# State products on the quarters of the matmul array, rows turned by the transpose form, and scatters spread, in a kernel of retention and two layers of experts

## The chip, the cores and the metric

The kernel runs on one core of one Trainium2 chip. The metric is the device time of one execution in microseconds (us), as the median of several runs. A core has TensorE (matmuls, PE in the profile; its weight loads have a row of their own, PEld), VectorE (DVE), ScalarE (ACT), GpSimd (POOL) and SyncE (SP), which here only issues transfers. TensorE takes a stationary operand (the weights) from SBUF into its array, streams a moving operand past it and writes to PSUM, which has 8 banks of 512 float32 values for each of 128 partitions.

## The reference

Inputs are q, k and v of shape (8, 8, 576, 64) in float32 and two layers of 8 experts (512 to 1024 to 512). The first step is retention, attention without a softmax and with a decay of its own for each head:

```python
scores = (q @ k^T) / sqrt(64)
ret    = scores * where(i >= j, gamma[h] ** (i - j), 0)
x      = ret @ v                      # then as 4608 rows of 512
logits = x @ w_gate                   # expert of a row: argmax; weight: its softmax
out[t] = gate_w * sigmoid(x @ w_output_gate)[e] * relu(x @ w1[e]) @ w2[e]
```

A second layer of experts of the same form follows, with a bias on its logits that depends on a modality, and without the output gate.

## The kernel before

Two stages follow each other. The first, `attention_and_routing`, computes the retention, the logits of the first layer and each row's place, and scatters the rows to DRAM by expert. The second, `experts`, runs both layers of experts; the diff doesn't touch it.

The first stage works on 36 chunks of 128 rows. Each sequence of 576 has four chunks of 128 and a rest of 64; the rests of two sequences make one chunk, the tail. So of 36 chunks 8 are the first of a sequence, 24 have one chunk before them and 4 are tails. The decay is taken out of the products by scaling v by gamma to the power of minus its position (`vs`, on GpSimd) and the result by gamma to the power of its position (`gx`). What earlier chunks of a sequence add is carried in a state `Sb`, a 64x64 matrix for each head, summed up from chunk to chunk. All of this is in float32; a float32 matmul shows as two rows of PE and two weight loads.

For a chunk TensorE does, by line:

- `scores` (277): 8 products of 64 rows by 128 columns into `pa`, one head each; the two heads of a pair stand on the two halves of the partitions.
- `kv` (284): 8 products with 64 output partitions into `pS`, from which `state` (293 on DVE, 295 on ACT for a first chunk) makes `Sb` in two instructions of 64 partitions. `Sb` has a 128x128 block for a pair of heads, whose two 64x64 corners off the diagonal are zeros, set once.
- `qS` (302): 4 products of the whole array, a pair's block of `Sb` as weights against q, into `po`, one bank. A tail has two such sets of 64 columns, one for each sequence.
- `av` (322): 8 products into the two halves of `po`'s partitions, on top of `qS`.
- `out` (326, DVE) scales `po` into `og`, which has head dimensions in its partitions. `turned` (331) multiplies `og` as weights with `iw`, an identity of 128 columns and 16 columns of both gates beside it, so that one set of 4 float32 products into `px` (two banks) gives the rows and, in four parts, their logits.

Then ACT takes the sum of squares (336), DVE adds up the four parts of the logits (339) and makes a power of two of the sum (345, 349), ACT and DVE write the row as two float16 halves (353, 356).

GpSimd scales v (269, `vs`), zeroes what lies above the diagonal of the scores (317, two instructions a chunk) and issues the scatters of finished rows (178), one a chunk.

Chunks are routed in 9 groups of 4, 5, 4, 5, 4, 5, 4, 3 and 2. `route` is a chain of some 15 small steps on DVE with a few on the other engines (lines 191 to 234; `oh` is 201, `zz` 203). The order of everything is written out: `PLAN` gives each step of chunk i a time i + offset, in chunks, and the program is issued sorted by it; every engine works off its part in that order. On TensorE that is scores of i, `turned` of i - 2, `qS` and `av` of i - 1, `kv` of i. A group's scatters stand at the end of its route plus 0.225, and 0.428 chunks apart.

Of the kernel before, what the change touches and what calls it, by code (L numbers as in the profile page):

```python
# [13 lines left out]
F32 = mybir.dt.float32  # L14
I32 = mybir.dt.int32
AF = mybir.ActivationFunctionType
ALU = mybir.AluOpType
AX = mybir.AxisListType

B, H, S, HD = 8, 8, 576, 64  # L20
D, F, E = 512, 1024, 8
N = B * S
P = 128
C = 128
NCH = 4
# [4 lines left out]
TOK0 = 8192.0  # L30
WS = 64.0
NT = N // P
IW = P + 2 * E

PLAN = {
    "vs": -1.3, "S": 0.0, "x": 2.03, "am0": 0.05, "am1": 0.06, "qS": 1.06, "av": 1.1, "kv": 0.2, "cut0": 0.21, "cut1": 0.22, "oe": 1.3, "Sb": 0.5,
# [2 lines left out]
GATES = -5.2, -1.440, -2.415, 1.091  # L39
WARM = 15  # L40
STEPS, RANKS, STEP, HURRY = 15, 10, 0.1684, {27: 0.1, 31: 0.055, NT - 2: 0.04}
SCATTER = 0.225, 0.428
HALVES = (38.2, 38.3, 38.32, 38.34, 38.36, 38.38, 38.4, 38.42), 43.0
READY = 11

# [1 line left out]
def const_tables():  # L47
    g = 1.0 - 2.0 ** (-5.0 - np.arange(H, dtype=np.float64))
    p = np.arange(P)
    cols = {}  # L50
    for c in range(NCH + 1):
        at = c * C + (p if c < NCH else p % 64) - S // 2
        cols[f"gv{c}"] = g[None, :] ** -at[:, None].astype(np.float64)
    tok = np.zeros((P, NT))
    for b in range(B):
        for c in range(NCH):
            tok[:, tile_index(b, c)] = b * S + c * C + p
    for bp in range(B // 2):
        tok[:, tile_index(2 * bp, NCH)] = 2 * bp * S + 512 + p + 512 * (p >= 64)
    cols["tok"] = tok - TOK0  # L60
    cols["desc"] = np.tile(8.0 - np.arange(E), (P, 1))
    cols["e8"] = np.tile(np.arange(E, dtype=np.float64), (P, 1))
    cols["e40"] = np.tile(R // P * np.arange(E), (P, 1))
    cols["eR"] = np.tile(R * np.arange(E), (P, 1))
    cols["eP"] = np.tile(R * np.arange(E) + P, (P, 1))
    cols["suf"] = np.tile((np.arange(E)[:, None] <= np.arange(E)[None, :]).reshape(1, 64), (P, 1))
    off, at = {}, 0
    for k, v in cols.items():
        off[k] = (at, at + v.shape[1])
        at += v.shape[1]  # L70
    gx = np.zeros((NCH + 1, 2, HD, 4, P))
    for c in range(NCH + 1):
        at = c * C + (p if c < NCH else p % 64) - S // 2
        gx[c] = (g.reshape(4, 2).T[:, None, :, None] ** at.astype(np.float64)) / 8.0
    return np.concatenate(list(cols.values()), 1).astype(np.float32), off, gx.reshape(NCH + 1, P, 4 * P).astype(np.float32)


def tile_index(b, c):

    return (b // 2) * 9 + ((b % 2) * NCH + c if c < NCH else 8)  # L80


def attention_and_routing(tc, st, I, K):

    nc = tc.nc
    pool = lambda n, b: st.enter_context(tc.tile_pool(name=n, bufs=b))
    one, two, three = pool("one", 1), pool("two", 2), pool("three", 3)
    psum = lambda n, b: st.enter_context(tc.tile_pool(name=n, bufs=b, space=bass.MemoryType.PSUM))
    ps = psum("ps", 1)
    rows = dram_disjoint_views(K["xs1"], NT)  # L90
# [8 lines left out]
    id16, mt = (one.tile([P, P], F16, tag=n, name=n) for n in ("id16", "mt"))  # L99
# [18 lines left out]
                rest[w] = r  # L118

    wgf = one.tile([P, 4, 16], F32, tag="wgf", name="wgf")  # L120
    iw = one.tile([P, 4, IW], F32, tag="iw", name="iw")
    wg2f = one.tile([P, 4, 8], F32, tag="wg2f", name="wg2f")
    mi = one.tile([NT, P, 2], I32, tag="mi", name="mi")
    tokm = one.tile([P, NT, XM - 1], F32, tag="tokm", name="tokm")
# [5 lines left out]
        nc.sync.dma_start(mi, I["modality"].bitcast(I32).rearrange("t (p w) -> t p w", w=2))  # L130

    def gate_weights():
        nc.vector.tensor_copy(iw[:, :, 0:P], id16.unsqueeze(1).to_broadcast([P, 4, P]))
        nc.vector.tensor_copy(iw[:, :, P:IW], wgf)
        split3((K["wg2"], wg2f, 8))

    def modalities():

        mf = one.tile([NT, P], F32, tag="mf", name="mf")
        nc.vector.tensor_copy(mf, mi[:, :, 0])  # L140
        pm = ps.tile([P, 1024], F32, tag="px", bufs=2, name="pm_mod")
        id32 = one.tile([NT, NT], F32, tag="id32", name="id32")
        nc.vector.tensor_copy(id32, id16[0:NT, 0:NT])
        nc.tensor.transpose(pm[:, 0:NT], mf, id32)
        nc.vector.tensor_copy(tokm[:, :, 0], col("tok"))
        nc.vector.memset(tokm[:, :, 1:2], 1.0)
        nc.vector.memset(tokm[:, :, 10:11], 0.0)
        return pm[:, 0:NT]
# [88 lines left out]
    gx = [one.tile([P, 512], F32, tag=f"gx{c}", name=f"gx{c}") for c in range(NCH + 1)]  # L237
# [3 lines left out]

    HALF = (slice(0, 64), slice(64, 128))

    states = [one.tile([P, 4, P], F32, tag=f"Sb{n}", name=f"Sb{n}") for n in range(7)]
    for x in states:
        nc.gpsimd.memset(x, 0.0)

    class Chunk:

# [36 lines left out]

        def state(self):
            self.Sb = states[order.index(self) % 7]
            for r in range(2):
                at = lambda x: x[HALF[r], :, r * HD:(r + 1) * HD]  # L290
                new = self.pS[HALF[r], 0:256].rearrange("p (a d) -> p a d", a=4)
                if self.c:
                    nc.vector.tensor_tensor(at(self.Sb), new, at(self.before[0].Sb), op=ALU.add)
                else:
                    nc.scalar.activation(at(self.Sb), new, AF.Copy)

        def qS(self):
            self.po = ps.tile([P, 4, P], F32, tag="po", name=f"po{self.tag}")
            for m, bf in enumerate(self.before):
                part = HALF[m] if self.tail else slice(0, P)  # L300
                for hp in range(4):
                    nc.tensor.matmul(self.po[:, hp, part], bf.Sb[:, hp], self.pairs("q")[:, hp, part], start=(m == 0 and hp == 0), stop=False)

        def a_full(self, r):

# [11 lines left out]
                nc.gpsimd.affine_select(out=d4, in_=d4, pattern=[[0, 4], [1, C]], compare_op=ALU.is_ge, fill=0.0, base=0, channel_multiplier=-1)  # L317

        def av(self):
            for hp in range(4):  # L320
                for r in range(2):
                    nc.tensor.matmul(self.po[HALF[r], hp, :], self.vs[:, 2 * hp + r, :], self.aa[r][:, hp * P:(hp + 1) * P], start=(not self.c and hp == 0), stop=(hp == 3))

        def out(self):
            self.og = two.tile([P, 4, P], F32, tag="og", name=f"og{self.tag}")
            nc.vector.tensor_tensor(self.og, self.po, gx[self.c].rearrange("p (h i) -> p h i", h=4), op=ALU.mult)  # L326

        def turned(self):
            px = ps.tile([P, 1024], F32, tag="px", bufs=2, name=f"px{self.tag}").rearrange("p (h t) -> p h t", h=4)
            for hp in range(4):  # L330
                nc.tensor.matmul(px[:, hp, 0:IW], self.og[:, hp, :], iw[:, hp, :], start=True, stop=True)  # L331
            self.x, self.xl = px[:, :, 0:P], px[:, :, P:IW]

        def squares(self):
            sq = two.tile([P, 512], BF16, tag="sq", name=f"sq{self.tag}")
            nc.scalar.activation(four(sq), self.x, AF.Square, accum_out=self.of("ss"))

        def logits(self):
            nc.vector.tensor_reduce(self.group.lg[:, self.place], self.xl.rearrange("p h e -> p e h"), axis=AX.X, op=ALU.add)

        def of(self, n):
            return getattr(self.group, n)[:, self.place:self.place + 1]
# [7 lines left out]

        def x_hi(self):
            self.xr = self.group.xrow[:, self.place, 0:512].bitcast(F16)
            nc.scalar.activation(four(self.xr[:, 0:512]), self.x, AF.Identity, scale=self.of("sc"))

        def x_lo(self):
            nc.vector.scalar_tensor_tensor(four(self.xr[:, 512:1024]), self.x, self.of("sc"), four(self.xr[:, 0:512]), op0=ALU.mult, op1=ALU.subtract)

    four = lambda a: a.rearrange("p (h d) -> p h d", h=4)
    order = []
    for bp in range(B // 2):  # L360
        order += [Chunk(2 * bp + bb, c) for bb in range(2) for c in range(NCH)] + [Chunk(2 * bp, NCH)]
# [14 lines left out]
    add = lambda when, f, *a_: plan.append((when, len(plan), f, a_))  # L376
# [7 lines left out]
    for gr in groups:  # L384
        last = max(gr.start + n + PLAN["lg"] for n, x in enumerate(gr.items))
        chain = route(gr)
        for k in range(STEPS):
            last += HURRY.get(gr.start, STEP)
            if k == RANKS and gr.start < NT - 2:
                last = int(last - 0.045) + 1.045  # L390
            add(last, next, chain, None)
        for n, x in enumerate(gr.items):
            add(last + SCATTER[0] + n * SCATTER[1], scatter, x)
    def counts():

        pm = ps.tile([P, 512], F32, tag="pS", name="pm_cnt")
# [16 lines left out]
    for when, f in zip(GATES, (gate_loads, gate_weights, lambda: mod.append(modalities()), token_data)):  # L413
        add(when, f)
# [984 lines left out]
def laid_out(inputs):  # L1399

    a = {n: inputs[n] for n in _INS}
    for n in "kv":
        a[n] = by_tile(inputs[n].transpose(0, 2, 1, 3)).reshape(NT, P, D)
    for n, x in (("q", "q"), ("dk", "k")):
        a[n] = by_tile(inputs[x].transpose(0, 2, 1, 3)).reshape(NT, P, 4, P).transpose(0, 3, 2, 1).reshape(NT, P, D)
    a["modality"] = by_tile(inputs["moe2_modality_id"].reshape(B, S))
    rows = lambda w: w.reshape(4, P, E).transpose(1, 0, 2)
    a["gates"] = np.concatenate([rows(inputs["moe_w_gate"]), rows(inputs["moe_w_output_gate"])], 2)
    a["gate2"] = rows(inputs["moe2_w_gate"])
    return a  # L1410

# [16 lines left out]
```

## Time and profile before

| | us |
|---|---|
| median of 3 runs | 1028.07 (1027.68 to 1029.19) |
| the profiled execution, its own time | 1029.08 |
| its span in the trace | 1026.6 |

The trace is of one execution. Its span runs from the first to the last instruction, and 2.5 us of the execution's own time lie outside it. A line of the profile's groups names source line, engine, operation, the tiles that it writes and reads, their shape and how many there were. A matmul's row begins when its moving operand may stream and ends with the last result, so rows overlap and what a matmul costs is read from the start of one row to the start of the next. Brackets behind a row tell how long its engine had been idle and what ended that.

### The profile page before, as it was taken

How to read it: one execution, taken by the hardware profiler on the slowest of the kernel's cores; microseconds unless marked ns; L12 is line 12 of the kernel's file. 1: busy time of each engine (PE TensorE's matmuls, PEld its weight loads, DVE VectorE, ACT ScalarE, POOL GpSimd, SP SyncE). 2: the span in 40 equal slices, each digit the busy share in tenths (PEclk: the TensorE clock that was granted, in tenths of full speed). 3: DMA queues.
4: the chain of work that ended last, by engine and by line, in shares of the span. 5: the costliest groups of instructions: out<-in, count | busy, mean ns of one | idle time of the engine just before them, and what ended most of it. 6: DMA issues, size and time to landing. Idle time of an engine off the chain costs nothing. (4 is left out here: it accounts for less than half of the span.)

```text
span 1026.6 us, 23918 instructions
## 1 busy us (share of the span) xinstructions
PE 984.4 (96%) x8529; PEld 708.7 (69%) x8529; DVE 465.6 (45%) x1420; ACT 358.6 (35%) x701; POOL 234.8 (23%) x308
## 2 busy tenths in 40 slices
PE   8998999399999999999999999999999999999996
PEld 6998898357667676767666767666776666776673
DVE  4666766666565656565656565323111111111111
ACT  3564554344444444343534343223111121111111
POOL 6566655510121111111112111101100101100110
PEclk9999999789999999999999999999999999999998
DMA  8887875279739383747665564361222211112100
GB/s 326 302 295 245 276 246 177 96 238 269 187 60 244 76 234 84 190 114 172 216 169 142 111 185 97 113 173 53 52 42 51 72 34 52 53 41 62 52 31 24
DMA packets 180256, 145.10 MB, mean 141 GB/s; under 512 B 136569, under 2 KB 136733, under 8 KB 180128
## 3 DMA queue, kind: packets, MB, share of 16 engines
q1 hardware_dynamic: 171168, 114.89, 42.2%
q0 software_dynamic: 8960, 28.62, 7.4%
q8 instruction: 67, 1.10, 0.4%
q14 instruction: 61, 0.50, 0.2%
HBM read 80.46 MB, written 33.92 MB: 111 GB/s over the span
## 5 line engine op out<-in xcount | busy, mean ns | idle before, releaser
L991 PE MATMUL ph<-xT,wb 128*128 128x256 f16 (+2 forms) x1344 | 338.0, 262 | 0.1
L993 PE MATMUL ph<-xT,wb 128*128 128x256 f16 (+2 forms) x1344 | 338.0, 262 | 0.0
L992 PE MATMUL ph<-xT,wb 128*128 128x256 f16 (+2 forms) x1344 | 338.0, 262 | 0.0
L1205 DVE SCALAR_TENSOR_TENSOR hT<-ph,hT 128x512 f16<-128x512 f32 (+2 forms) x168 | 105.8, 637 | 332.2 <-DVEq L457 332.1
L1001 PE MATMUL py<-wb,hT 128*128 128x512 f16 x608 | 230.4, 379 | 0.0
L1000 PE MATMUL py<-wb,hT 128*128 128x512 f16 x608 | 230.3, 379 | 0.0
L999 PE MATMUL py<-wb,hT 128*128 128x512 f16 x608 | 230.3, 379 | 0.0
L1093 ACT ACTIVATE hT<-ph 128x512 f16<-128x512 f32 (+2 forms) x168 | 92.4, 551 | 200.9 <-ACTq L457 200.7
L991 PEld LDWEIGHTS ph<-xT,wb 128*128 128x128 f16 x1344 | 131.3, 98 | 16.3 <-issue 0.4
L992 PEld LDWEIGHTS ph<-xT,wb 128*128 128x128 f16 x1344 | 131.3, 98 | 16.0
L993 PEld LDWEIGHTS ph<-xT,wb 128*128 128x128 f16 x1344 | 131.4, 98 | 12.7
L1331 POOL DMA_INDIRECT out_dram<-yo,idxo x37 | 35.9, 969 | 334.3 <-POOLq L457 334.3
L1001 PEld LDWEIGHTS py<-wb,hT 128*128 128x128 f16 x608 | 59.4, 98 | 71.8
L999 PEld LDWEIGHTS py<-wb,hT 128*128 128x128 f16 x608 | 59.3, 98 | 63.4
L1000 PEld LDWEIGHTS py<-wb,hT 128*128 128x128 f16 x608 | 59.4, 98 | 63.2
L1320 POOL TENSOR_SCALAR idx<-v_pos 128x1 int32<-128x1 f32 x39 | 22.2, 570 | 325.8 <-POOLq L457 325.8
L469 DVE SCALAR_TENSOR_TENSOR wb<-stg,wb 128x2048 f16<-128x2048 f32 x38 | 86.9, 2287 | 10.2 <-DVEq L457 9.7
L1087 ACT ACTIVATE yo<-py,v_gcol 128x512 f32<-128x512 f32 x37 | 25.4, 688 | 168.2 <-ACTq L457 168.2
L1070 ACT ACTIVATE wb<-stg 128x2048 f16<-128x2048 f32 x38 | 72.3, 1902 | 0.9 <-ACTq L457 0.9
L1324 POOL DMA_INDIRECT xs<-x2row,idx x39 | 44.4, 1137 | 37.5 <-POOLq L457 37.5
L331 PE MATMUL px<-iw,og 128*128 128x144 f32 x288 | 46.0, 304 | 6.7 <-DVE og L326 6.7
L1084 ACT ACTIVATE x2row<-py,v_s 128x512 f16<-128x512 f32 x39 | 26.8, 687 | 71.6 <-ACTq L457 71.6
(152 smaller groups left out, 977.0 us busy)
## 6 DMA issues: line engine op xcount, KB each, us to landing
stg<-in_moe_w_dram SPq DMA_DIRECT2D x38, 1024.0 KB, 5.0
qn<-in_q_dram SPq DMA_DIRECT2D x36, 256.0 KB, 5.0
dkn<-in_dk_dram SPq DMA_DIRECT2D x36, 256.0 KB, 5.1
vn<-in_v_dram SPq DMA_DIRECT2D x36, 256.0 KB, 5.1
kn<-in_k_dram SPq DMA_DIRECT2D x32, 256.0 KB, 5.1
xs<-zero SPq DMA_DIRECT2D x8, 262.0 KB, 2.2
xs<-zero SPq DMA_DIRECT2D x8, 258.0 KB, 2.4
w0s<-in_moe_w_dram SPq DMA_DIRECT2D x8, 256.0 KB, 5.8
```

The source lines that it names most:

```text
L331: nc.tensor.matmul(px[:, hp, 0:IW], self.og[:, hp, :], iw[:, hp, :], start=True, stop=True)
L469: r = fn(*a, **kw).then_inc(self.sem, 1)
L991: pe.matmul(o, w1(P_, 0)[:, c, fs], xT[s][:, c, cs], start=(c == 0), stop=False)
L992: pe.matmul(o, w1(P_, 0)[:, c, fs], xT[s][:, 4 + c, cs], start=False, stop=False)
L993: m = pe.matmul(o, w1(P_, 1)[:, c, fs], xT[s][:, c, cs], start=False, stop=(c == 3))
L999: pe.matmul(py[b], hT[:, 0, f, bs], w2(P_, 0)[:, f, :], start=(f == 0), stop=False)
L1000: pe.matmul(py[b], hT[:, 0, f, bs], w2(P_, 1)[:, f, :], start=False, stop=False)
L1001: m = pe.matmul(py[b], hT[:, 1, f, bs], w2(P_, 0)[:, f, :], start=False, stop=(f == 7))
L1070: ac.activation(wb[P_ % 2][:, 0, 2048 * c:2048 * c + 2048], stg[:, 2048 * c:2048 * c + 2048], AF.Copy, scale=WS).then_inc(T["cv_full"])
L1093: ac.activation(hT[:, 0, 2 * g:2 * g + 2, cs], ph[g][:, :, cs], AF.Relu).then_inc(T["hh_full"])
L1205: stt(hT[:, 1, 2 * g:2 * g + 2, cs], ph[g][:, :, cs], 0.0, hT[:, 0, 2 * g:2 * g + 2, cs], op0=ALU.max, op1=ALU.subtract).then_inc(T["h_full"])
L1324: po.indirect_dma_start(out=xs2, out_offset=bass.IndirectOffsetOnAxis(ap=idx[b], axis=0), in_=x, in_offset=None, bounds_check=E * R - 1, o ...
```

## The change

- `Sb` has 4 x 64 columns with no zeros; `state` is one instruction of 128 partitions by 256.
- `qS` becomes 8 products of 64x64 (16 in a tail), each on one quarter of the array: r picks the half of its rows (and of q's and `Sb`'s partitions), s the half of its columns (and of `po`'s partitions). `po` takes two banks, one for each r. `av` and `out` follow that layout; `gx` and the gates' rows are arranged for it on the host.
- `turned` is four transposes of `og` against a float32 identity `idf` into `px`, which is one bank, and four products of `og` with the 16 gate columns that add up in a bank `pl` of their own. `logits` is a copy of 16 columns.
- A group's scatters stand 0.9 chunks apart, from the group that starts at chunk 22 on 0.428 as before.
- The zeroing of the states at the start goes.

```diff
-SCATTER = 0.225, 0.428
+SCATTER, APART, LATE = 0.225, (0.9, 0.428), 22
...
-    gx = np.zeros((NCH + 1, 2, HD, 4, P))
+    gx = np.zeros((NCH + 1, 2, HD, 2, 2, P))
+    by_place = g.reshape(2, 2, 2).transpose(1, 2, 0)[:, None, :, :, None]
...
-    iw = one.tile([P, 4, IW], F32, tag="iw", name="iw")
+    idf = one.tile([P, P], F32, tag="idf", name="idf")
...
-    states = [one.tile([P, 4, P], F32, tag=f"Sb{n}", name=f"Sb{n}") for n in range(7)]
-    for x in states:
-        nc.gpsimd.memset(x, 0.0)
+    states = [one.tile([P, 4 * HD], F32, tag=f"Sb{n}", name=f"Sb{n}") for n in range(7)]
...
-            for r in range(2):
-                at = lambda x: x[HALF[r], :, r * HD:(r + 1) * HD]
-                new = self.pS[HALF[r], 0:256].rearrange("p (a d) -> p a d", a=4)
-                if self.c:
-                    nc.vector.tensor_tensor(at(self.Sb), new, at(self.before[0].Sb), op=ALU.add)
-                else:
-                    nc.scalar.activation(at(self.Sb), new, AF.Copy)
+            new = self.pS[:, 0:4 * HD]
+            if self.c:
+                nc.vector.tensor_tensor(self.Sb, new, self.before[0].Sb, op=ALU.add)
+            else:
+                nc.scalar.activation(self.Sb, new, AF.Copy)
+
+        def at(self, r, s, u):
+
+            return self.po[HALF[s], 512 * r + P * u:512 * r + P * (u + 1)]
 
         def qS(self):
-            self.po = ps.tile([P, 4, P], F32, tag="po", name=f"po{self.tag}")
+            self.po = ps.tile([P, 1024], F32, tag="po", name=f"po{self.tag}")
             for m, bf in enumerate(self.before):
                 part = HALF[m] if self.tail else slice(0, P)
-                for hp in range(4):
-                    nc.tensor.matmul(self.po[:, hp, part], bf.Sb[:, hp], self.pairs("q")[:, hp, part], start=(m == 0 and hp == 0), stop=False)
+                for u in range(2):
+                    for r, s in ((0, 0), (1, 1), (0, 1), (1, 0)):
+                        hp = 2 * u + s
+                        nc.tensor.matmul(self.at(r, s, u)[:, part], bf.Sb[HALF[r], hp * HD:(hp + 1) * HD], self.pairs("q")[HALF[r], hp, part],
+                                         start=(m == 0 and u == 0), stop=False)
...
         def turned(self):
-            px = ps.tile([P, 1024], F32, tag="px", bufs=2, name=f"px{self.tag}").rearrange("p (h t) -> p h t", h=4)
+            px = ps.tile([P, 512], F32, tag="px", bufs=2, name=f"px{self.tag}")
+            pl = ps.tile([P, 512], F32, tag="pl", name=f"pl{self.tag}")
+            turned = px.rearrange("p (u s r d) -> p r u s d", u=2, s=2, r=2)
+            for n in range(4):
+                nc.tensor.transpose(turned[:, n // 2, n % 2], self.og[:, n, :], idf)
             for hp in range(4):
-                nc.tensor.matmul(px[:, hp, 0:IW], self.og[:, hp, :], iw[:, hp, :], start=True, stop=True)
-            self.x, self.xl = px[:, :, 0:P], px[:, :, P:IW]
+                nc.tensor.matmul(pl[:, 0:2 * E], self.og[:, hp, :], wgf[:, hp, :], start=(hp == 0), stop=(hp == 3))
+            self.x, self.xl = px, pl[:, 0:2 * E]
...
         def logits(self):
-            nc.vector.tensor_reduce(self.group.lg[:, self.place], self.xl.rearrange("p h e -> p e h"), axis=AX.X, op=ALU.add)
+            nc.vector.tensor_copy(self.group.lg[:, self.place], self.xl)
...
         for n, x in enumerate(gr.items):
-            add(last + SCATTER[0] + n * SCATTER[1], scatter, x)
+            add(last + SCATTER + n * APART[gr.start >= LATE], scatter, x)
```

## Rows read from the trace of the kernel before

**Rows 1.** Busy time by stretch: length, PE, PEld, DVE, ACT, POOL, granted clock, DMA share, GB/s.

```profile
20.00:75.00 55.00, 55.00 (x773) 50.82 (x769) 36.29 (x112) 31.67 (x71) 33.00 (x42) 1.00 0.87 306
75.00:92.00 17.00, 14.18 (x167) 12.93 (x163) 14.48 (x35) 6.10 (x16) 8.84 (x12) 0.90 0.64 221
```

**Rows 2.** TensorE's timeline: start us, us, what; chunks at 31, 39 to 46, 50 us.

```profile
30.92 1.25 PE L331 MATMUL px<-iw,og 128*128 128x144 f32 x8
32.09 1.09 PE L322 MATMUL po<-a,vs 128*64 128x128 f32 x16
...
39.32 1.25 PE L331 MATMUL px<-iw,og 128*128 128x144 f32 x8
...
41.69 1.09 PE L322 MATMUL po<-a,vs 128*64 128x128 f32 x16
42.61 0.64 PE L284 MATMUL pS<-vs,kn 128*64 128x64 f32 x16
43.18 1.16 PE L277 MATMUL pa<-qn,dkn 64*128 64x128 f32 x16
44.27 1.25 PE L331 MATMUL px<-iw,og 128*128 128x144 f32 x8
45.35 1.05 PE L302 MATMUL po<-qn,Sb 128*128 128x128 f32 x8
46.34 1.09 PE L322 MATMUL po<-a,vs 128*64 128x128 f32 x16
...
49.54 1.89 PE L302 MATMUL po<-qn,Sb 128*128 128x64 f32 x16
51.36 1.09 PE L322 MATMUL po<-a,vs 128*64 128x128 f32 x16
```

**Rows 3.** The same view where lines 322 and 284 meet, early in the stage.

```profile
15.11 0.28 PE L284 MATMUL pS<-vs,kn 128*64 128x64 f32 x2
15.21 0.27 PE L322 MATMUL po<-a,vs 128*64 128x128 f32 x1
```

**Rows 4.** By line: duration ns min/median/max, first and last start, forms.

```profile
L144 PEld LDWEIGHTS pm_mod<-id,mf x1: 135/135/135, 6.9 to 6.9; 36*128 36x128 f32 x1
L144 PE MATMUL pm_mod<-id,mf x1: 248/248/248, 6.9 to 6.9; 36*128 36x36 f32 x1
...
L277 PEld LDWEIGHTS pa<-qn,dkn x576: 182/188/188, 8.1 to 179.3; 64*128 64x128 f32 x192
L277 PE MATMUL pa<-qn,dkn x576: 272/272/373, 8.1 to 179.4; 64*128 64x128 f32 x192
...
L284 PE MATMUL pS<-vs,kn x512: 219/222/270, 9.9 to 178.3; 128*64 128x64 f32 x171
```

**Rows 5.** TensorE's timeline in the second stage: float16, 256 columns.

```profile
211.31 0.27 PE L992 MATMUL ph<-xT,wb 128*128 128x256 f16 x1
211.42 0.27 PE L993 MATMUL ph<-xT,wb 128*128 128x256 f16 x1
```

**Rows 6.** The timeline around two halts of TensorE, 75 to 90 and 128 us.

```profile
75.75 1.25 PE L331 MATMUL px<-iw,og 128*128 128x144 f32 x8
...
77.70 3.79 DVE L201 TENSOR_TENSOR oh<-wq,m 128x32 f16<-128x32 f32 x1
...
80.40 1.04 POOL L269 TENSOR_TENSOR vs<-vn,cst 128x512 f32<-128x512 f32 x1
...
82.85 1.25 PE L331 MATMUL px<-iw,og 128*128 128x144 f32 x8 [2.38 <-DVE og L326]
...
89.91 1.25 PE L331 MATMUL px<-iw,og 128*128 128x144 f32 x8
...
128.19 1.53 PE L331 MATMUL px<-iw,og 128*128 128x144 f32 x8 [2.09 <-DVE og L326]
```

**Rows 7.** GpSimd's groups, 17 to 188 us: busy us, mean ns, idle before.

```profile
L317 POOL TENSOR_SCALAR_AFFINE_SELECT a<-a 128x512 f32<-128x512 f32 x62 | 38.1, 641 | 28.4 <-ACT a L311 28.2
...
L178 POOL DMA_INDIRECT xs<-xr,pi x32 | 32.0, 1001 | 36.7 <-DVE xr L234 28.3 <-issue 5.0 <-ACT xr L353 3.1
```

More of the change, by code (lines that the diff above doesn't have):

```diff
@@ L32 @@
 NT = N // P
-IW = P + 2 * E
 PLAN = {
@@ L70, in const_tables @@
         at += v.shape[1]
-    gx = np.zeros((NCH + 1, 2, HD, 4, P))
+    gx = np.zeros((NCH + 1, 2, HD, 2, 2, P))
+    by_place = g.reshape(2, 2, 2).transpose(1, 2, 0)[:, None, :, :, None]
     for c in range(NCH + 1):
         at = c * C + (p if c < NCH else p % 64) - S // 2
-        gx[c] = (g.reshape(4, 2).T[:, None, :, None] ** at.astype(np.float64)) / 8.0
+        gx[c] = (by_place ** at.astype(np.float64)) / 8.0
     return np.concatenate(list(cols.values()), 1).astype(np.float32), off, gx.reshape(NCH + 1, P, 4 * P).astype(np.float32)
@@ L132, in gate_weights @@
     def gate_weights():
-        nc.vector.tensor_copy(iw[:, :, 0:P], id16.unsqueeze(1).to_broadcast([P, 4, P]))
-        nc.vector.tensor_copy(iw[:, :, P:IW], wgf)
+        nc.vector.tensor_copy(idf, id16)
         split3((K["wg2"], wg2f, 8))
@@ L140, in modalities @@
         nc.vector.tensor_copy(mf, mi[:, :, 0])
-        pm = ps.tile([P, 1024], F32, tag="px", bufs=2, name="pm_mod")
+        pm = ps.tile([P, 512], F32, tag="px", bufs=2, name="pm_mod")
         id32 = one.tile([NT, NT], F32, tag="id32", name="id32")
@@ L319, in av @@
         def av(self):
-            for hp in range(4):
+            for u in range(2):
                 for r in range(2):
-                    nc.tensor.matmul(self.po[HALF[r], hp, :], self.vs[:, 2 * hp + r, :], self.aa[r][:, hp * P:(hp + 1) * P], start=(not self.c and hp == 0), stop=(hp == 3))
+                    for s in range(2):
+                        hp = 2 * u + s
+                        nc.tensor.matmul(self.at(r, s, u), self.vs[:, 2 * hp + r, :], self.aa[r][:, hp * P:(hp + 1) * P], start=(not self.c and u == 0), stop=(u == 1))
         def out(self):
             self.og = two.tile([P, 4, P], F32, tag="og", name=f"og{self.tag}")
-            nc.vector.tensor_tensor(self.og, self.po, gx[self.c].rearrange("p (h i) -> p h i", h=4), op=ALU.mult)
+            halves = lambda a: a.rearrange("p (r x) -> p r x", r=2)
+            nc.vector.tensor_tensor(self.og.rearrange("p (r u) t -> p r (u t)", r=2), halves(self.po)[:, :, 0:2 * P], halves(gx[self.c]), op=ALU.mult)
         def turned(self):
-            px = ps.tile([P, 1024], F32, tag="px", bufs=2, name=f"px{self.tag}").rearrange("p (h t) -> p h t", h=4)
+            px = ps.tile([P, 512], F32, tag="px", bufs=2, name=f"px{self.tag}")
[3 more added lines that the diff above has]
+                nc.tensor.transpose(turned[:, n // 2, n % 2], self.og[:, n, :], idf)
             for hp in range(4):
-                nc.tensor.matmul(px[:, hp, 0:IW], self.og[:, hp, :], iw[:, hp, :], start=True, stop=True)
-            self.x, self.xl = px[:, :, 0:P], px[:, :, P:IW]
+                nc.tensor.matmul(pl[:, 0:2 * E], self.og[:, hp, :], wgf[:, hp, :], start=(hp == 0), stop=(hp == 3))
+            self.x, self.xl = px, pl[:, 0:2 * E]
         def squares(self):
             sq = two.tile([P, 512], BF16, tag="sq", name=f"sq{self.tag}")
-            nc.scalar.activation(four(sq), self.x, AF.Square, accum_out=self.of("ss"))
+            nc.scalar.activation(sq, self.x, AF.Square, accum_out=self.of("ss"))
         def logits(self):
-            nc.vector.tensor_reduce(self.group.lg[:, self.place], self.xl.rearrange("p h e -> p e h"), axis=AX.X, op=ALU.add)
+            nc.vector.tensor_copy(self.group.lg[:, self.place], self.xl)
         def of(self, n):
@@ L352, in x_hi @@
             self.xr = self.group.xrow[:, self.place, 0:512].bitcast(F16)
-            nc.scalar.activation(four(self.xr[:, 0:512]), self.x, AF.Identity, scale=self.of("sc"))
+            nc.scalar.activation(self.xr[:, 0:512], self.x, AF.Identity, scale=self.of("sc"))
         def x_lo(self):
-            nc.vector.scalar_tensor_tensor(four(self.xr[:, 512:1024]), self.x, self.of("sc"), four(self.xr[:, 0:512]), op0=ALU.mult, op1=ALU.subtract)
-    four = lambda a: a.rearrange("p (h d) -> p h d", h=4)
+            nc.vector.scalar_tensor_tensor(self.xr[:, 512:1024], self.x, self.of("sc"), self.xr[:, 0:512], op0=ALU.mult, op1=ALU.subtract)
     order = []
@@ L1407, in laid_out @@
     rows = lambda w: w.reshape(4, P, E).transpose(1, 0, 2)
-    a["gates"] = np.concatenate([rows(inputs["moe_w_gate"]), rows(inputs["moe_w_output_gate"])], 2)
+    placed = lambda w: w.reshape(2, 2, 2, HD, E).transpose(1, 3, 2, 0, 4).reshape(P, 4, E)
+    a["gates"] = np.concatenate([placed(inputs["moe_w_gate"]), placed(inputs["moe_w_output_gate"])], 2)
     a["gate2"] = rows(inputs["moe2_w_gate"])
```

## Prediction

> **What bounds the kernel now.** First I read the busy time by stretch [rows 1]. From 20 to 75 us, in the first stage, TensorE is busy for 55.00 of 55.00 us at the full clock (granted 1.00, so 2.4 GHz), while VectorE has 36.29, GpSimd 33.00 and ACT 31.67. So this stage goes at TensorE's pace, and the diff touches no other. From 75 to 92 us it is not so: 14.18 of 17.00, at a mean clock of 0.90.
>
> Second, TensorE's timeline [rows 2], where a step costs from its start to the next one's start. A normal chunk is av 41.69 to 42.61 = 0.92, kv 0.57, scores 1.09, turned 44.27 to 45.35 = 1.08, qS 45.35 to 46.34 = 0.99: 4.65 us. With a group's rank products in between it is 4.95 (39.32 to 44.27). A tail's qS, twice as many rows of half the columns, takes 49.54 to 51.36 = 1.82. In a first chunk, without qS, turned is followed at once by av and takes 1.17 (30.92 to 32.09) and not 1.08. The 0.09 more is what it costs to go from a whole-array step to one on halves of the array; qS ends in such a change too. So its 8 rows take (0.99 - 0.09) / 8 = 0.112 each, and the tail's 16 take (1.82 - 0.09) / 16 = 0.108 though they stream 64 columns and not 128. Those rows are bound by loading 128 columns of float32 weights, not by streaming.
>
> Third, what two halves of the array do. av has 16 rows of 128 columns in 0.92 us: two at a time, 8 steps of some 0.11 and a first load of weights. kv's 16 rows of 64 columns take 0.57, (0.57 - 0.09) / 8 = 0.06 a step. The halves don't keep step by construction: kv starts on one half at 15.11 before the other has begun its last av row at 15.21 [rows 3]. So each part of the array works off its own rows.
>
> Fourth, the halts [rows 6]. `oh`, 32 elements wide, lasts 3.79 us and ends at 81.49, just after GpSimd's `vs` ends at 81.44. VectorE's `og` stands behind it in order, and TensorE waits 2.38 us for that; after the wait the clock falls, to a mean of 0.90 over the stretch [rows 1]. From 75.75 to 89.91 are 14.16 us for a normal chunk and one with ranks, 4.65 + 4.95 = 9.60: the halt costs 4.56. A second, with 2.09 of waiting at 128.19, is put at 4.56 x 2.09 / 2.38 = 4.0. In the old order four or five scatters stand within two chunks, 2.3 a chunk, and GpSimd then needs 2 x 0.64 + 1.04 + 2.3 x 1.0 = 4.6 us a chunk [rows 6, 7], as long as the chunk itself. It runs without a break, and by these rows a VectorE step like `oh`, which reads two operands from SBUF, gets through only in a break.
>
> **The change part by part.**
>
> *qS on quarters.* Each quarter has 2 products, so 4 rows of 128 columns, and 64 columns of weights, half the load. No row shows four quarters at once. The bounds come from av: if the four work off their own rows as its two halves do, 4 steps of 0.11; if only two run at a time, 8 steps. I take the first, by [rows 3] and because each half of rows and each half of columns is already seen at work in scores and av. Added are 0.09 for the change into av as before, 0.05 for the first weights (below) and 0.02 for four starts: 0.44 + 0.16 = 0.60 against 0.99, -0.39 in each of 24 chunks. In a tail each quarter has 8 rows of 64 columns: 8 x 0.06 + 0.16 = 0.64 against 1.82, -1.18, four times. With two at a time: 1.04 and 1.12.
>
> *Turned.* The gates' products keep `og` as weights, so their 8 rows cost the load that binds a tail's qS: 8 x 0.108 = 0.86, nearly the old step. The transposes come on top. The one transpose of the trace [rows 4] has one row where every other float32 product has two. Its weights take 135 ns, against 183 and more for 128 columns elsewhere; a first row that waits for its weights is 373 - 272 = 101 ns longer with 128 columns, so some 50 here. That leaves 198 of its 248 for 36 columns. Ordinary rows go from 222 ns at 64 columns to 272 at 128, 0.8 a column, or 200 at 36: the same pace. So 128 columns cost 0.11, one row each. Bounds: float16 streams 256 columns in 0.11 [rows 5], which makes 0.055; and two rows like other products make 0.22. I take 0.11, the only row of that form. Sum: 4 x 0.11 + 0.05 + 0.86 = 1.35. The next change costs nothing more, since 16 columns have left the array long before the next load is due. So +0.27 in 28 chunks and 1.35 - 1.17 = +0.18 in the 8 first ones.
>
> The Trainium skill ("TensorE: Matmul & The Clock Gate", Terms) says that the transpose mode is 4 times faster for float32 than a plain product. By that a transpose would cost a quarter of two rows, near 0.055, and the sum would be lower by 4 x 0.055 in each chunk; the only row here speaks for half and not a quarter.
>
> *State, out, logits.* One VectorE instruction where there were two, and a copy where there was a sum. VectorE isn't the bound; these cost and give nothing as long as TensorE is. `out` still has kv and scores, 0.57 + 1.09 us, as cover before the next turned. If that cover is gone, each such chunk waits. The logits' single bank `pl` is free a whole chunk before it is needed. The zeroing at the start lies ahead of the first loads: nothing.
>
> *Scatters.* 0.9 chunks apart they are 1.1 a chunk: with 5.0 / 32 = 0.16 of issue each, 2 x 0.64 + 1.04 + 1.1 x 1.16 = 3.6 of some 4.5 us, so GpSimd waits for ACT's scores again in each chunk and VectorE gets its break. Both halts above belong to groups before chunk 22; I take them as gone, -8.6. Bounds: nothing gone, or new halts (below). Scatters from chunk 22 on are as before.
>
> *Sum.* 24 x (-0.39 + 0.27) = -2.9; tails 4 x (-1.18 + 0.27) = -3.6; first chunks 8 x 0.18 = +1.4; halts -8.6: -13.7. The profiled execution's own time is 1029.08 (its span 1026.6 and 2.5 around it), 1.0 above the median of 1028.07. So the median becomes 1014.4, put at 1014.5.
>
> **Rivals.**
>
> *Transposes twice as fast* (0.055, the float16 pace): 36 x 4 x 0.055 = 7.9 less, 1006.5. For it: the weights of the one transpose load in half the usual excess. Against: its 248 ns.
>
> *The halts stay*, because one scatter a chunk is enough to close GpSimd's breaks: 1014.5 + 8.6 = 1023. For it: all that covers `og` after av is 1.66 us, so a block of `oh` well short of 3.79 us would do.
>
> *Two quarters at a time*: 24 x 0.44 + 4 x 0.48 = 12.5 more, 1027, no difference that can be measured.
>
> *More halts, the other side.* Scatters spread over four chunks now lie under the route of the following group, which they did only for two groups before 22. If `oh` or `zz` is caught in each of the five groups 4, 9, 13, 18 and 22, that is 5 x 4.3 = 21 us where I count none: 1035. It decides at four of them: 17 more make 1031.7. Against it: the order leaves GpSimd 0.9 us idle in each chunk, and a scatter is preceded by a gap of its issue.
>
> *A transpose of two rows*: 36 x 4 x 0.11 = 15.8 more, 1030, about the edge.
>
> **How the numbers follow.** Chances: forecast 0.38, fast transposes 0.18, halts stay 0.18, two quarters 0.10, more halts 0.10, two rows or something else that is dear 0.06. 0.2% is 2.1 us, about what a measurement of this kernel can tell from no change. Faster are the first three and some of the fourth, 0.76; same 0.08; slower 0.16. The predicted time is the likeliest case's, 1014.5; the range takes in the first four, from 1004 (fast transposes with the loads a little better hidden) to 1027.
>
> **What would show it.** Right: the rows of 302 start four within some 30 ns and qS takes 0.60; line 331's successor has 4 rows 0.11 apart and 8 rows 0.108 apart; `oh` and `zz` stay under 2 us before chunk 22 and TensorE has no wait of over 1 us for `og` there; the second stage is as long as before. Wrong: qS near 1.04, or transposes with eight rows, or TensorE waiting for `og` in more places than two, or the stage ending later while its matmuls are shorter, with VectorE or GpSimd as what it waits for.

## The result, and the profile after

The changed kernel takes 1012.87 us (median of 4 runs, 1011.63 to 1014.00) against 1028.63 of the kernel before on the same chip (4 runs, 1027.68 to 1029.93): a ratio of 0.9833 [0.9819, 0.9848]. The forecast was 1014.5. In the profiled execution the span goes from 1026.6 to 1009.9 us, 16.7 less; the medians are 15.8 apart.

First the stretches of [rows 1] again: length, PE, PEld, DVE, ACT, POOL, granted clock, DMA share, GB/s.

```profile
20.00:75.00 55.00, 55.00 (x923) 50.78 (x921) 33.26 (x108) 30.11 (x69) 35.26 (x45) 1.00 0.91 315
75.00:92.00 17.00, 17.00 (x298) 15.51 (x297) 10.25 (x39) 8.65 (x20) 12.55 (x16) 1.00 0.84 277
```

TensorE is still busy without a break at the full clock from 20 to 75 us, and now from 75 to 92 as well, where it had 14.18 of 17.00 us and a mean clock of 0.90. VectorE, ACT and GpSimd all have room, so the stage goes at TensorE's pace in both stretches. TensorE's timeline, which answers to [rows 2]:

```profile
31.69 0.66 PE L338 MATMUL px<-idf,og 128*128 128x128 f32 x4
...
33.08 1.09 PE L326 MATMUL po<-a,vs 128*64 128x128 f32 x16
...
40.22 0.66 PE L338 MATMUL px<-idf,og 128*128 128x128 f32 x4
...
41.73 0.67 PE L303 MATMUL po<-qn,Sb 64*64 64x128 f32 x16
...
44.91 0.66 PE L338 MATMUL px<-idf,og 128*128 128x128 f32 x4
45.40 0.96 PE L340 MATMUL pl<-wgf,og 128*128 128x16 f32 x8
46.30 0.67 PE L303 MATMUL po<-qn,Sb 64*64 64x128 f32 x16
46.89 1.09 PE L326 MATMUL po<-a,vs 128*64 128x128 f32 x16
...
50.40 0.69 PE L303 MATMUL po<-qn,Sb 64*64 64x64 f32 x32
51.02 1.09 PE L326 MATMUL po<-a,vs 128*64 128x128 f32 x16
```

From start to start, qS takes 46.30 to 46.89 = 0.59 and a tail's 50.40 to 51.02 = 0.62. The four transposes take 44.91 to 45.40 = 0.49 and the gates' eight rows 45.40 to 46.30 = 0.90. A chunk with ranks is 40.22 to 44.91 = 4.69, where it was 4.95; a normal one, from qS to qS, 41.73 to 46.30 = 4.57, where it was 4.65. Cut down to 46.28 to 46.32 us, the same view has one line of four products:

```profile
46.30 0.34 PE L303 MATMUL po<-qn,Sb 64*64 64x128 f32 x4
```

The four quarters' first rows start within 0.02 us of each other and run together. By line, ns (min/median/max), beside [rows 4]: a transpose has one row (x144 for 36 chunks), and its weights load in 141 ns, against 192 for the same `og` in the gates' products.

```profile
L338 PEld LDWEIGHTS px<-idf,og x144: 137/141/143, 18.0 to 172.2; 128*128 128x128 f32 x144
L338 PE MATMUL px<-idf,og x144: 272/273/329, 18.0 to 172.3; 128*128 128x128 f32 x144
...
L340 PEld LDWEIGHTS pl<-wgf,og x288: 190/192/192, 18.4 to 173.1; 128*128 128x128 f32 x144
```

Where the first halt was [rows 6], the timeline now has the following. GpSimd waits for ACT's scores before each pair of cuts (the brackets), `oh` and `zz` last 0.19 and 0.52 us, and the next `turned` starts without a wait, 4.57 us after the one before.

```profile
75.38 0.66 PE L338 MATMUL px<-idf,og 128*128 128x128 f32 x4
...
76.08 0.19 DVE L200 TENSOR_TENSOR oh<-wq,m 128x32 f16<-128x32 f32 x1
76.22 1.22 POOL L319 TENSOR_SCALAR_AFFINE_SELECT a<-a 128x512 f32<-128x512 f32 x2 [0.57 <-ACT a L313]
...
76.97 0.52 DVE L202 TENSOR_TENSOR zz<-lg,oh 128x32 f32<-128x32 f32 x1
...
79.95 0.66 PE L338 MATMUL px<-idf,og 128*128 128x128 f32 x4
```

**The balance.** A measure that every run below has is the stage, in its one profiled execution, from the first `turned` to the last: before 16.97 to 188.51 = 171.54 us, after 18.00 to 171.96 = 153.96, so 17.6 less. The stage's first `turned` is 1.0 later (the first scores wait 2.38 us for `dkn` instead of 0.97; close_scatters below, which starts with the same steps, has it at 16.80, so this is the run's and not the change's), the way from the last `turned` to the experts' first matmul is 0.8 shorter, and the second stage takes 820.4 instead of 819.8: 17.6 - 1.0 + 0.8 - 0.6 = 16.8, the span's 16.7 but for rounding.

Of the 17.6, halts are 12.1. The kernel before had three. The forecast saw two, 4.56 and one put at 4.0. At the second, the two steps from one `turned` to the next take 6.81 + 6.59 instead of 4.65 + 4.95, which is 3.8 more. The third lies behind chunk 22, in rows of before that stand nowhere yet:

```profile
166.26 1.25 PE L331 MATMUL px<-iw,og 128*128 128x144 f32 x8
...
168.22 1.62 DVE L203 TENSOR_TENSOR zz<-lg,oh 128x32 f32<-128x32 f32 x1
...
168.73 1.06 POOL L269 TENSOR_TENSOR vs<-vn,cst 128x512 f32<-128x512 f32 x1
...
173.10 2.05 PE L331 MATMUL px<-iw,og 128*128 128x144 f32 x8 [0.62 <-DVE og L326]
...
179.57 1.25 PE L331 MATMUL px<-iw,og 128*128 128x144 f32 x8
```

179.57 - 166.26 = 13.31 for two steps that need 4.65 + 4.95: 3.7. After the change none of the three is there, and 17.6 - 12.1 = 5.5 is what the matmuls themselves gave. Part of a halt's price is the clock: in the kernel before, the granted clock is at half (1.2 GHz) for 3.4 us from 84.6, 129.0 and 173.4 us, behind each of the three.

### The profile page after: what moved, and what is told of

Its sections match the earlier page's. It is cut to its first block, busy times and chain, and to the rows that moved or that the text cites. A ratio compares the mean times of both kernels' runs of the same rounds, so it can differ in the third digit from the quotient of the medians.

```text
span 1009.9 us, 24673 instructions
## 1 busy us (share of the span) xinstructions
PE 972.9 (96%) x8929; PEld 699.1 (69%) x8929; DVE 444.7 (44%) x1395; ACT 352.3 (35%) x693; POOL 232.0 (23%) x301
## 5 line engine op out<-in xcount | busy, mean ns | idle before, releaser
L1328 POOL TENSOR_SCALAR idx<-v_pos 128x1 int32<-128x1 f32 x39 | 24.4, 625 | 324.9 <-POOLq L465 324.9
L313 ACT ACTIVATE a<-pa 128x512 f32<-128x512 f32 x64 | 34.7, 593 | 38.2 <-PE pa L274 38.0
```

## The experiments

Theory at the outset: the new matmuls cost what the forecast says, and the halts went because the scatters were spread. Rivals: the halts went because of the other parts; or a transpose is no cheaper than a product. The runs were made on three chips, each beside the kernel before, whose medians there are 1031.38, 1031.03 and 1039.13 us; ratios are to that. "Stage" is first to last `turned` in the one profiled execution, so medians are compared on one chip only.

| run | stage us | median us | ratio [95%] |
|---|---|---|---|
| close_scatters | 158.41 | 1015.44 | 0.9849 [0.9832, 0.9865] |
| spread_only | 167.52 | 1027.73 | 0.9972 [0.9961, 0.9984] |
| plain_products | 171.6 | 1032.57 | 1.0022 [1.0005, 1.0039] |
| turned_only | 175.37 | 1035.26 | 1.0049 [1.0032, 1.0067] |
| joint_quarters | 157.97 | 1014.04 | 0.9835 [0.9810, 0.9860] |
| joint_close | 159.57 | 1021.56 | 0.9912 [0.9889, 0.9936] |
| close_two_states | 157.79 | 1017.92 | 0.9879 [0.9855, 0.9903] |
| after_again | 153.97 | 1013.86 | 0.9835 [0.9807, 0.9862] |
| joint_early | 159.95 | 1017.38 | 0.9787 [0.9753, 0.9820] |
| vs_on_vector | 172.31 | 1031.69 | 0.9919 [0.9887, 0.9950] |
| after_beside | 158.31 | 1019.06 | 0.9812 [0.9780, 0.9844] |

The first four share a chip, so do the next four, and the last three.

**close_scatters**: the changed kernel with the old distance.

```diff
-SCATTER, APART, LATE = 0.225, (0.9, 0.428), 22
+SCATTER, APART, LATE = 0.225, (0.428, 0.428), 22
```

> The changed kernel with all scatters 0.428 chunks apart, as before. Theory (the spread removed the halts): the halts before chunk 22 come back, about 4 us each; two of them make 1021, three 1025. Rival (the halts went because VectorE has less to do and its logits no longer wait for ACT's squares, so that the small routing steps fall elsewhere): within 2 us of 1013.

The stage is 4.45 us longer than the changed kernel's. Two halts come back, at about half their old price together, and the third does not. The timeline around the first:

```profile
74.18 0.66 PE L338 MATMUL px<-idf,og 128*128 128x128 f32 x4
...
74.95 0.98 POOL L177 DMA_INDIRECT xs<-xr,pi  x1 [0.30 <-issue]
...
75.76 3.46 DVE L202 TENSOR_TENSOR zz<-lg,oh 128x32 f32<-128x32 f32 x1
...
75.94 1.06 POOL L266 TENSOR_TENSOR vs<-vn,cst 128x512 f32<-128x512 f32 x1
...
76.94 1.22 POOL L319 TENSOR_SCALAR_AFFINE_SELECT a<-a 128x512 f32<-128x512 f32 x2
...
78.13 1.04 POOL L266 TENSOR_TENSOR vs<-vn,cst 128x512 f32<-128x512 f32 x1
...
80.22 0.66 PE L338 MATMUL px<-idf,og 128*128 128x128 f32 x4 [1.41 <-DVE og L331]
...
86.42 0.66 PE L338 MATMUL px<-idf,og 128*128 128x128 f32 x4
```

`zz` begins 0.18 us before `vs` and lasts until the second `vs` ends (75.76 + 3.46 = 79.22; 78.13 + 1.04 = 79.17): GpSimd runs vs, cut, cut, vs without a bracket, so without a wait. TensorE waits 1.41 us where it had waited 2.38; the granted clock falls to half (1.2 GHz) for 3.4 us from 81.4. The two steps take 86.42 - 74.18 = 12.24 instead of 4.56 + 4.69, +2.99. At the second halt the wait is 1.41 too but the clock stays, and it costs 1.47. So in this kernel the spread is worth 4.5 us of the stage, not 8.6. (The medians, 1015.44 and 1012.87, come from two chips and are 2.6 apart.)

**spread_only**: the kernel before with the changed kernel's scatters.

```diff
-SCATTER = 0.225, 0.428
+SCATTER, APART, LATE = 0.225, (0.9, 0.428), 22
...
-            add(last + SCATTER[0] + n * SCATTER[1], scatter, x)
+            add(last + SCATTER + n * APART[gr.start >= LATE], scatter, x)
```

> The kernel before with the scatters 0.9 chunks apart up to chunk 22, and nothing else. Theory: the two halts before 22 go, 8.6 us less, 1020; the third, whose scatters stay as they were, remains. Rival (lighter VectorE work did it): no change, 1028.6, with long oh and zz steps.

The stage is 4.0 us shorter. The two halts shrink to 1.3 us each, but in the groups that start at chunks 4, 13 and 22 two steps now take 5.02 + 5.52 instead of 4.65 + 5.0, 0.9 each, and the third halt stays: 6.84 + 5.46, +2.7. The clock stays at full here from 20 to 185 us; the third halt has the same waits as before (0.95 and 0.62 us), so that 2.7 instead of 3.7 is put down to the clock. The rival of new halts was real, at a fifth of the price that I gave it.

**turned_only**: the kernel before with the new transposes (one bank), the logits apart (their own bank) and the copy; whole-array qS, old state and old scatters.

```diff
-                nc.tensor.matmul(px[:, hp, 0:IW], self.og[:, hp, :], iw[:, hp, :], start=True, stop=True)
+                nc.tensor.transpose(px[:, hp * P:(hp + 1) * P], self.og[:, hp, :], idf)
+            for hp in range(4):
+                nc.tensor.matmul(pl[:, 0:2 * E], self.og[:, hp, :], wgf[:, hp, :], start=(hp == 0), stop=(hp == 3))
```

> The kernel before with the transposes and the logits apart, and nothing else (old state blocks, old scatters). By the trace of the changed kernel turned takes 1.385 for 1.085: 36 x 0.30 less about 1 us at the ranks = 10 us more. Theory (the spread removed the halts): the halts stay, 1038. Rival (logits that don't wait for the squares remove them): 1038 - 12 = 1026.

On its own this part makes the kernel slower. In TensorE's timeline `turned` takes 47.50 to 48.80 = 1.30, and the qS behind it 48.80 to 49.87 = 1.07, where it had 0.99:

```profile
47.50 0.66 PE L331 MATMUL px<-idf,og 128*128 128x128 f32 x4
...
48.80 1.14 PE L301 MATMUL po<-qn,Sb 128*128 128x128 f32 x8
49.87 1.09 PE L321 MATMUL po<-a,vs 128*64 128x128 f32 x16
```

Normal chunks are 4.95 (+0.30). The halts fall to 3.6, 2.0 and 1.8, 7.3 in all, 4.8 less than before, which is why the whole is +0.5% and not near +0.9%. Part of the 4.8 is the clock, which here falls behind the first halt alone, two times fewer; at 1.0 us a fall (spread_only) to 1.5 (2.99 - 1.47 in close_scatters) that is an estimated 2 to 3 us.

**plain_products**: the changed kernel with the transposes as products with the same identity.

```diff
-                nc.tensor.transpose(turned[:, n // 2, n % 2], self.og[:, n, :], idf)
+                nc.tensor.matmul(turned[:, n // 2, n % 2], self.og[:, n, :], idf, start=True, stop=True)
```

> The changed kernel with each transpose as a plain product with the identity: two rows of 0.112 each and a first load of 128 columns (0.10 for 0.05). 36 x (8 x 0.112 + 0.10 - 0.49) = 18 us more, 1031, if TensorE sets the pace of every chunk. Rival (part of turned lies in time in which TensorE would have waited for another engine): clearly less, 1020 to 1025.

The eight rows take 46.73 to 47.73 = 1.00 instead of 0.49, and the stage is 17.6 us longer, 0.49 a chunk for 36 chunks. A transpose is worth half a product here. And what TensorE's work grew by went into the stage one for one: no part of `turned` lay in time in which it would have waited.

```profile
46.73 1.16 PE L338 MATMUL px<-idf,og 128*128 128x128 f32 x8
47.73 0.96 PE L340 MATMUL pl<-wgf,og 128*128 128x16 f32 x8
```

So the parts don't add up: each alone takes only some of the 12 us. The next question was what in the rest of the change makes halts cheaper, and whether the dearer `turned` can be had back.

**close_two_states**: close_scatters with the state added in two instructions of 64 partitions, as before the change.

```diff
-                nc.vector.tensor_tensor(self.Sb, new, self.before[0].Sb, op=ALU.add)
+                for r in range(2):
+                    nc.vector.tensor_tensor(self.Sb[HALF[r]], new[HALF[r]], self.before[0].Sb[HALF[r]], op=ALU.add)
```

> The changed kernel with the scatters at their old distance and the state added in two instructions of 64 partitions again, 0.42 us more of VectorE in a chunk. Theory (what VectorE has left over in a chunk decides how much of its held steps reaches TensorE): the waits for og go from 1.4 us to about 2.2 each and the third halt comes back, 1017 to 1018.5 us. Rival (the state has no part in it): two halts as with the close scatters alone, 3.0 and 1.5 us, no third, 1015.4 us.

My theory of VectorE's spare time falls: with 0.42 us more work a chunk the stage is 0.6 us *shorter* than with the close scatters alone. The time, 1017.92, lies within what the theory gave, and the third halt, 2.3, is back as it said; but the first two are 0.6 and 0.9, cheaper where it had them dearer, so the hit is luck. The timeline, at the place of the first:

```profile
77.29 0.99 POOL L177 DMA_INDIRECT xs<-xr,pi  x1 [0.30 <-issue]
...
77.56 0.18 DVE L202 TENSOR_TENSOR zz<-lg,oh 128x32 f32<-128x32 f32 x1
...
78.29 1.06 POOL L266 TENSOR_TENSOR vs<-vn,cst 128x512 f32<-128x512 f32 x1
...
79.29 1.22 POOL L320 TENSOR_SCALAR_AFFINE_SELECT a<-a 128x512 f32<-128x512 f32 x2
...
80.48 1.04 POOL L266 TENSOR_TENSOR vs<-vn,cst 128x512 f32<-128x512 f32 x1
...
81.36 1.35 DVE L211 TENSOR_TENSOR cum<-cum,seen 128x8 f16<-128x8 f16 x1
81.47 1.21 POOL L320 TENSOR_SCALAR_AFFINE_SELECT a<-a 128x512 f32<-128x512 f32 x2
...
82.66 1.03 POOL L266 TENSOR_TENSOR vs<-vn,cst 128x512 f32<-128x512 f32 x1
```

GpSimd's unbroken run is there as before. But `zz` now falls under a scatter and lasts 0.18 us; it is `cum`, later in the route, that is caught, and only for 1.35, until the cuts end. By these rows it is not the amount of VectorE's work that counts but which step of the route begins just ahead of a run of vs and cuts, a matter of a few tenths of a microsecond: `zz` starts 0.73 us ahead of `vs` here and 0.18 in close_scatters. On this chip after_again beside it is 1013.86: 4.1 us less, as the stages say (3.8).

> The changed kernel beside the others on one chip: 1012 to 1014 us, a ratio of 0.983 to 0.986. Against it the close scatters with two state instructions show what the two together are worth.

**vs_on_vector**: a direct test of who holds `oh` and `zz`, the kernel before with one word changed.

```diff
-            nc.gpsimd.tensor_tensor(self.vs, self.heads("v"), col(f"gv{self.c}").unsqueeze(2).to_broadcast([P, 8, HD]), op=ALU.mult)
+            nc.vector.tensor_tensor(self.vs, self.heads("v"), col(f"gv{self.c}").unsqueeze(2).to_broadcast([P, 8, HD]), op=ALU.mult)
```

> The kernel before with the scaled v made on VectorE instead of GpSimd, nothing else. Theory (a step of VectorE that reads two operands from SBUF is held while GpSimd runs without a break, and the scatters, vs and the two cuts make such a run): no step held for 3.6 us, PE's halts of 12 us gone; vs costs VectorE 0.7 us a chunk that it has left over: 1016 to 1020 us. Rival (the hold comes from the scatters' own descriptor work): the holds and halts stay, 1028 us or more. Rival (VectorE becomes the bound or og comes late for vs): new waits in each chunk, above 1033 us.

The holds are gone: by line, `oh` and `zz` have maxima of 0.41 us, with the scatters as close as ever.

```profile
L201 DVE TENSOR_TENSOR oh<-wq,m x9: 174/200/407, 41.7 to 195.0; 128x32 f16<-128x32 f32 x4, 128x40 f16<-128x40 f32 x3, 128x24 f16<-128x24 f32 x1, 128x16 f16<-128x16 f32 x1
```

TensorE has no wait of over 0.62 us between the second `turned` and 180 us. The stage of 172.31 us is no measure against the 171.54 of before, which is from another chip. Its second `turned` comes 7.41 us after the first:

```profile
18.48 2.29 PE L331 MATMUL px<-iw,og 128*128 128x144 f32 x8 [2.36 <-DVE og L326]
...
25.89 1.25 PE L331 MATMUL px<-iw,og 128*128 128x144 f32 x8
```

There TensorE is busy without a break, but its granted clock is at half from 17.5 to 24.3 us, and at the end stands a wait that all three kernels of this chip have (see joint_early). From the second `turned` to the 34th, away from both, it is 151.1 us against 158.0 in the kernel before. Of the 12.1 us of halts, 5.2 are paid back in and behind the chunks with ranks, where VectorE, which now has `vs` to do, makes TensorE wait (steps of 5.1 to 5.5 us instead of 5.0, and of 4.8 instead of 4.2). The medians say the same: 1031.69 against 1039.13 on this chip, 7.4 less, where the forecast, 1016 to 1020, was 8 to 12 less than 1028. So the theory stands; the forecast left out what VectorE pays.

**joint_quarters**: the changed kernel with `turned` again as one product of 144 columns. Two banks for each `px` no longer fit beside `po`'s two, so two chunks share three banks; the heads are paired 4r + hp on the host so that rows come out in order.

```diff
-            for n in range(4):
-                nc.tensor.transpose(turned[:, n // 2, n % 2], self.og[:, n, :], idf)
-            for hp in range(4):
-                nc.tensor.matmul(pl[:, 0:2 * E], self.og[:, hp, :], wgf[:, hp, :], start=(hp == 0), stop=(hp == 3))
+            for n in range(4):
+                nc.tensor.matmul(px[:, n, 0:IW], self.og[:, n, :], iw[:, n, :], start=True, stop=True)
```

> The changed kernel with the turned rows and the logits again in one product of 144 columns, as before the change; the quarters, the state in one instruction and the spread scatters stay. Theory (TensorE sets the pace and the new turned rows cost it 0.30 us a normal chunk, 0.2 a first one and 0.13 a chunk with ranks): normal chunks of 4.26 us, the stage about 8.5 us shorter than in the changed kernel, 1004 us. Rival (the logits that come apart and early are what keeps the halts away): halts of some 5 us in all come back beside the shorter chunks, 1009 us. Rival (GpSimd, at 3.1 us a chunk, or the loads become the bound): chunks stay at 4.5 us, 1012 us.

Chunks shrink to 4.36 us, yet the stage is 4.0 us longer than the changed kernel's. (Over the whole kernel the two are even, 1014.04 and 1013.86 for after_again: the second stage of joint_quarters is 2.4 us shorter, 819.0 against 821.4, for which no run shows a reason.) The timeline where the stage loses:

```profile
52.42 1.25 PE L342 MATMUL px<-iw,og 128*128 128x144 f32 x8
...
53.60 1.09 PE L331 MATMUL po<-a,vs 128*64 128x128 f32 x16
...
54.92 0.68 DVE L336 TENSOR_TENSOR og<-po,gx 128x512 f32<-128x512 f32 x1
...
55.52 1.20 DVE L194 TENSOR_TENSOR dl<-lg,mx 128x40 f32<-128x40 f32 x1
...
56.64 0.74 DVE L367 SCALAR_TENSOR_TENSOR xr<-px,sc,xr 128x512 f16<-128x512 f32 x1
...
57.43 0.76 PE L342 MATMUL px<-iw,og 128*128 128x144 f32 x4 [1.18 <-DVE xr L367]
```

`og` is ready at 55.60, but the shared banks let `turned` begin only when the low halves of the chunk before have been read, at 57.38, and a held `dl` stands ahead of those. A joint product costs 52.42 to 53.60 = 1.18 here, so the new `turned` costs 0.21 more than it, not 0.31; within the stage, what pays for that is a `px` that is free in time.

**joint_close**: joint_quarters with the old scatters: the quarters and the one state instruction, with the shared banks besides.

```diff
-SCATTER, APART, LATE = 0.225, (0.9, 0.428), 22
+SCATTER, APART, LATE = 0.225, (0.428, 0.428), 22
```

> As joint_quarters, with the scatters at their old distance: the quarters and the one state instruction alone. Theory (halts need VectorE held and TensorE short of other work; with less work for VectorE in a chunk they are cheaper but there): two halts of 3 to 4 us each over joint_quarters, no third one, 1009 to 1011 us. Rival (the quarters have no part in the halts): all three halts as before the change, 12 us, 1028.6 less 14.1 = 1014.5 us. Rival (the quarters alone do away with them): as joint_quarters.

Two halts of 2.4 us, after waits of 2.37 each, and none of the waits of 1.18: the stage is 1.6 us longer. With the quarters too there are halts where the scatters are close, cheaper ones than the 4.56 and 3.8 of before; the clock stays at full behind them. The waits are for the low halves, `xr`, so the shared banks have a part in them. And the trace is of the shortest execution, 1016.26 us. The other four took 1021.27 to 1022.24, with a mean granted clock of 0.979 to 0.981 where the profiled one has 0.985; where they lost it no trace shows. So the median is 7.5 us above joint_quarters, none of the expected times came, and what a halt costs in one trace is not what it costs in every execution.

**joint_early** (with **after_beside** on its chip): joint_quarters with the low halves right behind `og`.

```diff
-    "sq": 2.1, "lg": 2.11, "rs1": 2.2, "rs2": 2.22, "xh": 2.25, "xl": 2.45,
+    "sq": 2.1, "lg": 2.11, "rs1": 2.2, "rs2": 2.22, "xh": 2.25, "xl": 2.305,
```

> joint_quarters with the low halves of x taken right behind og on VectorE, ahead of the routing steps, because the shared banks make each turned product wait for the low halves of the chunk before. Theory (the waits for xr were the only reason why its 4.36 us chunks did not shorten the stage): the waits of 1.18, 0.57 and 1.97 us go, the stage is 4 to 6 us shorter than in the changed kernel, 1007 to 1009 us. Rival (something else late, og or the cut scores, waits there instead): 1012 to 1014 us as joint_quarters.

> The changed kernel on the chip of these two: 1011.5 to 1014 us, a ratio near 0.984.

The waits of 1.18 us go, but 0.5 to 0.6 remain in each period of nine chunks; up to the 33rd of 36 `turned` it is ahead of after_beside by 0.6 us, and the stage's end loses that. The two ratios, 0.9787 [0.9753, 0.9820] and 0.9812 [0.9780, 0.9844], overlap: no version here is shown to beat the changed kernel. after_beside itself is 5 us above what was expected of it. On this chip all three kernels show one more wait of VectorE, of 2.5 to 3.2 us before `og` of the last chunk but one, which the trace puts down only to "remote"; its cause is open.

## Why the prediction was right

The time came out 1.6 us below the forecast. The terms, in the profiled execution:

| term | forecast | measured |
|---|---|---|
| qS on quarters, normal | 0.60 | 0.59 |
| qS, tail | 0.64 | 0.62 |
| `turned` | 1.35 | 1.39 (0.49 + 0.90) |
| `turned`, first chunk | 1.35 | 33.08 - 31.69 = 1.39 |
| matmuls in all | -5.1 | -5.5 |
| halts | -8.6 | -12.1 |

The stage lost 17.6 where the forecast had 13.7, 3.9 more. That the time shows only 1.6 of this is no merit of the forecast: 0.9 went outside the stage, 0.9 lie between the profiled executions and the medians, and the forecast counted from a median of 1028.07 where it is now 1028.63.

- *Quarters.* "If the four work off their own rows as its two halves do" holds: four rows start together and the step is gone in 0.59. The rival of two at a time is out.
- *Transposes.* One row each, 0.49 for four; the rivals of 0.055 and of two rows are out, the second by plain_products as well. The working that gave 0.11 from the one 36-column transpose was right. The factor of 4 that the prediction quotes from the Trainium skill ("TensorE: Matmul & The Clock Gate", Terms) is 2 here: four transposes take 0.49 us, four products with the identity 1.00.
- *"The next change costs nothing more"* was wrong, and small. Without quarters behind it `turned` takes 1.30 (turned_only), with them 1.39: the change from the whole array to quarters costs the 0.09 that such changes cost in [rows 2], and the rest of the sum, 1.35, was 0.05 too high. A chunk with ranks gained more than a normal one (0.26 instead of 0.12), which I had not told apart; that makes up for it.
- *The halts* are the step that was wrong in its reason and its size. "Both halts above ... I take them as gone" was said of the scatters' spread alone. In the changed kernel the spread is worth 4.5 us (close_scatters), in the kernel before 4.0 (spread_only). The new `turned` alone cut the halts by 4.8 (turned_only), an estimated 2 to 3 of that by the clock, and the other parts together also did away with a third halt, of 3.7, in a group whose scatters weren't moved; that one I had not listed at all. Had I read the trace to the end of the stage, the third would have stood in the sum as one that the spread can't remove. That it went all the same speaks against the spread as the only cause. By itself the spread would have given about half of the 8.6; that the term held is luck.
- *What a halt is* was read rightly, but for the scatters' part in it. VectorE steps that read two operands from SBUF are held by GpSimd's vs and cuts; a scatter alone doesn't hold them (`zz` under a scatter: 0.18 us). The scatters make GpSimd late, so that its next vs and cuts find their scores ready and run without waiting (no brackets). The Trainium skill ("SBUF — State Buffer", Who interferes with whom) says that a VectorE instruction with two SBUF inputs contends with a GpSimd instruction that reads SBUF. The traces agree, and vs_on_vector takes the cause away and the holds with it. For VectorE's 2-port modes the same section of the Trainium skill says that whoever issues first has the ports for the whole instruction; that sentence doesn't name steps like `zz`, which in close_scatters waited through four, 3.46 us, though its row begins first.
- *More halts* came in spread_only, three of 0.9 us, too cheap to turn the sign. In the changed kernel TensorE has no wait of over 0.8 us from the first `turned` to the last, but for the one of 3.43 at the end of after_beside. Holds remain in it (`dl` 1.16 us in three groups, `cum` 1.37 in one), too short to reach TensorE.

What stays open: why exactly the third halt vanishes with quarters and close scatters and comes back with two state instructions. The runs show that it hangs on tenths of a microsecond between the route and GpSimd, but no run moves one step by itself. Nor is it known when a hold begins and ends. It can begin before the row of the `vs` that it goes with: `oh` of [rows 6] starts at 77.70, under a scatter and 0.51 us before a `vs`, time enough for its usual 0.19 us, and is held; in close_scatters a `zz` starts at 178.08, as late under a scatter but with no `vs` behind it, and takes 0.17. And a step sometimes gets through between two GpSimd instructions, as `cum` did in close_two_states.

```profile
77.22 0.98 POOL L178 DMA_INDIRECT xs<-xr,pi  x1 [0.30 <-issue]
...
78.21 1.06 POOL L269 TENSOR_TENSOR vs<-vn,cst 128x512 f32<-128x512 f32 x1
```

## What to carry to other kernels

Price each matmul form from start to start, and price the changes of array shape between forms as terms of their own. A halt that comes from two engines' steps meeting is a matter of when they meet: list all such halts to the end of the stage, and don't credit their going to the one part of a change that was aimed at them until each part has been run alone. A cheaper form can be dear through the banks it needs: the quarters took a PSUM bank, and that, not the transposes' speed, is why `turned` was split; over the whole kernel the two forms came out even (1014.04 and 1013.86).

## What the runs showed that I had not expected

- A VectorE step of 32 elements a partition can be held for 3.5 to 3.8 us, through four GpSimd instructions in a row, by starting 0.2 to 0.5 us ahead of them; under a scatter the same step takes 0.18.
- A wait of TensorE of 1.41 us cost 1.47 in one place and 2.99 in another, because the granted clock fell to half for 3.4 us after one and not after the other.
- The fp32 transpose of 128x128 takes 0.11 us in one row, a product with the identity 0.25 us (1.00 for four).
